# Block-sparse attention and a routed expert layer on one core: where v's neighbour rows come from, and what is loaded ahead of an expert's weights

## The chip, the cores and the metric

The kernel runs on one core of a Trainium2 chip. The metric is device time in microseconds, the median of several executions; lower is better. One execution in each run is recorded by the hardware profiler, and the profile and trace quoted here are of that execution.

A core has TensorE (PE in the profile, its weight loads PEld), VectorE (DVE), ScalarE (ACT), GpSimd (POOL) and SyncE (SP). Transfers run on 16 DMA engines. In this kernel POOL issues every load from HBM that also converts fp32 to bf16, and SP issues the stores of the output.

## The reference

There are 4 batches, 8 heads, 768 positions and a head size of 64. Attention comes first. Each query sees the keys closer than 16 positions, and 24 summary keys, each the maximum over a block of 32 keys, whose value is the mean of the block:

```python
k_sum = k.reshape(B, H, nb, block, D).max(axis=3)
v_sum = v.reshape(B, H, nb, block, D).mean(axis=3)
scores_l = scale * np.matmul(q, k.transpose(0, 1, 3, 2))
mask_l = np.abs(pos[:, None] - pos[None, :]) < window        # window = 16
scores_s = scale * np.einsum('bhsd,bhnd->bhsn', q, k_sum) + np.log(block)
scores_all = np.concatenate([np.where(mask_l, scores_l, -1e9), scores_s], axis=-1)
a = softmax(scores_all)
attn = np.matmul(a, np.concatenate([v, v_sum], axis=2))
```

The heads are joined to x of 768 x 512 for each batch. Then one of 8 experts is chosen per batch, by the mean of x over its positions, and applied:

```python
logits = x.mean(axis=1) @ w_gate
e_idx = np.argmax(logits, axis=1)
h = np.maximum(x[b] @ w1[e], 0.0)          # 512 x 1024
out[b] = gate_w[b] * (h @ w2[e])           # 1024 x 512
```

So the weights of a batch can be fetched only when its attention is done.

## The kernel before

**Layout.** A batch is worked on in 4 pairs of heads, and a pair in 2 halves of 384 positions. The positions of a head lie in 12 blocks of 64. For each block the 64 queries are multiplied with 120 key rows: the block's own 64, 16 neighbours before (`R_PRE`), 16 behind (`R_POST`), and the 24 summaries (`R_SUM`). Bias matmuls with `mbias` and `ends` put a large negative number on what lies outside the window and on the neighbours that a head's first and last block do not have. `kaug` holds the keys in this form, `vblk` the values: rows 0 to 63 the block, 64 to 95 the two strips of neighbours, 96 to 119 the block sums, with extra columns of ones (32 for the sums) that give the denominator. Both exist twice, and batches alternate. `edges(i)` fills the constant parts.

**The steps.** `T_k` and `T_q` transpose a pair's keys and queries on TensorE (L241), and copies put them into `kaug` and `qT`. `K_rest` computes on DVE the block maxima (L271), the neighbour columns and the summary columns. `S_tile` does the biases (L350) and scores (L362), then the exponential on ACT (L372). `V_sum` sums v over blocks with matmuls (L300), `V_copy` spreads the sums over `vblk` on DVE (L315). `O_tile` multiplies weights and values (L386), then divides on DVE (L394, L397). `X_tile` transposes the result into `xT` (L413), and ACT sums its positions while it copies (L414). `gate(b)` computes the logits (L427), the maximum and its index, has POOL read the index, and issues the loads of w1 in four pieces (L453: 128, 128, 256 and 512 of 1024 columns) and w2 in two (L457). `H_chunk` is one 128 x 384 tile of the hidden layer (L492, 16 in a batch); `O_chunk` is half of a 128 x 512 output tile (L515, 12 in a batch), and every second one ends with a scaled copy and a store by SP (L531).

`warm` (L229) issues matmuls on zeros. `first_warm` has nine of 512 columns at the start; in batch 0 each score tile has two of 384 columns ahead of it, each output tile one, each sum two of 128.

**The order.** Nothing is planned by a tool: every engine works through its instructions in the order in which the program emits them. Batch 0 goes pair by pair (`a0`): transposes, sums, scores, outputs. From then on `weave(main, fill)` emits the chunks of one batch's expert layer with the attention steps of the next spread evenly between them: output chunks of batch b-1 with `scores(b + 1)`, hidden chunks of b with `values(b + 1)`, then `gate(b + 1)`. `values` starts with all sums and all four `V_copy`.

**The loads.** POOL's queue is in program order as well. At the start it holds keys, queries and values of batch 0 by pairs, then keys and queries of batch 1. The neighbour rows of batch 0's values are copied inside SBUF by SP, per pair (`halo`, L125 and L129, called from `V_sum`). For the other batches they come from HBM in two loads (`load_halos`, L114 and L118), and `gate` has a slot for them:

```python
nc.gpsimd.dma_start(w1_sb[:, :, fs], w1_src[:, :, fs])   # four pieces of w1
between()              # load_v of the next batch, two loads; load_halos, two
nc.gpsimd.dma_start(w2_sb[:, fs, :], w2_src[:, fs, :])   # two pieces of w2
```

So the order behind gate b is w1 of b, v of b + 1, w2 of b, and then (`load_k`, `load_q`) k and q of b + 2.

## Time and profile before

| | |
|---|---|
| median of 3 runs | 197.66 us (194.01, 206.86, 197.66) |
| the profiled execution, whole | 196.97 us |
| its span, first to last instruction | 194.9 us |
| mean granted TensorE clock | 0.939 |
| read from HBM | 38.00 MB |
| loads by POOL's queue | 19.00 MB as written to SBUF |

The span is what the views of the trace show; 2.07 us lie around it. Times in the views are microseconds from the start of the span. In the lists in order of time, a row has the start, the duration from the first to the last of its instructions, the engine, the line and the operation, the number of instructions, and in brackets the idle time before it and what ended it. A list of waits has for each pair the sum, the number, and the longest. Rows for a load have its size as written and the time from issue to landing.

### The profile page before, as it was taken

What the parts mean: (1) busy time and instruction counts of PE and PEld (TensorE: products, weight loads), DVE (VectorE), ACT (ScalarE), POOL (GpSimd) and SP (SyncE); (2) the same over time, 40 slices, a digit from 0 to 9 for tenths busy, and PEclk for the clock granted to TensorE, in tenths of its full rate; (3) what the DMA queues carried; (4) which work ended last, traced back from release to release, by engine and by line L of the source; (5) the groups of instructions that cost most, each with busy time, mean ns of one, the idle gap of its engine ahead of it and who ended that gap; (6) DMA issues with size and microseconds to landing.
All of it is one profiled execution on the core that took longest, in us unless ns stands there. A gap on an engine that the chain in (4) does not pass through costs nothing.

```text
span 194.9 us, 5234 instructions
## 1 busy us (share of the span) xinstructions
PE 165.7 (85%) x2242; PEld 95.9 (49%) x2257; DVE 92.6 (47%) x249; ACT 91.8 (47%) x187; POOL 47.1 (24%) x65
## 2 busy tenths in 40 slices
PE   7497988859987698989959998799969989979991
PEld 2355556547444365455525565455635644545440
DVE  5625475475036463768214853975257533121211
ACT  2132656748764066265831555466634651436120
POOL 7980000049700000497000000990000008000000
PEclk9998599975699799999996999999999999999999
DMA  4999950019999996399999991799998016999142
GB/s 45 149 172 222 215 93 3 0 20 139 158 101 95 203 207 120 57 151 187 194 123 200 206 175 62 111 157 203 177 157 148 3 55 105 168 274 156 54 161 108
DMA packets 57382, 26.00 MB, mean 133 GB/s; under 512 B 39696, under 2 KB 54288, under 8 KB 57360
## 3 DMA queue, kind: packets, MB, share of 16 engines
q0 software_dynamic: 52992, 19.00, 112.4%
q1 hardware_dynamic: 4368, 6.68, 11.4%
q8 instruction: 17, 0.28, 0.6%
q14 instruction: 5, 0.04, 0.1%
HBM read 38.00 MB, written 6.29 MB: 227 GB/s over the span
## 4 chain that ended last, share of the span: by engine, by line
DMA 36%; PE 35%; POOL 8%; issue 8%; DVE 5%; ACT 4%; POOLq 2%; SPq 0%; DVEq 0%; ACTq 0%
DMA vblk<-in_v_dram 27%; PE hps L492 12%; PE o_ps L515 8%; DMA w_sb<-in_moe_w_dram 6%; PE ops L386 5%; DMA vblk<-vblk 3%; POOL w_sb L453 3%; POOL vblk L104 3%; PE xps L413 2%; ACT xT L414 2%; PE vsps L300 2%; PE sc L229 1%; ACT qT L250 1%; ACT o_sb L530 1%; POOLq L439 1%
## 5 line engine op out<-in xcount | busy, mean ns | idle before, releaser
L492 PE MATMUL hps<-xT,w_sb 128*128 128x384 bf16 x256 | 50.7, 344 | 1.5 <-DMA w_sb<-in_moe_w_dram 1.3
L515 PE MATMUL o_ps<-w_sb,hT 128*128 128x512 bf16 x177 | 43.9, 380 | 1.6 <-issue 1.3
L453 POOL DMA_DIRECT2D w_sb<-in_moe_w_dram x16 | 12.0, 760 | 115.4 <-DVE grec L468 55.3
L503 ACT ACTIVATE hT<-hps 128x384 bf16<-128x384 f32 x48 | 23.4, 493 | 34.4 <-PE hps L492 34.1
L372 ACT ACTIVATE aT<-sc 128x768 bf16<-128x768 f32 x32 | 25.7, 811 | 16.1 <-PE sc L362 16.0
L492 PEld LDWEIGHTS <-w_sb 128*128 128x128 bf16 x256 | 23.6, 101 | 18.0 <-issue 3.1
L515 PEld LDWEIGHTS <-hT 128*128 128x128 bf16 x192 | 16.6, 98 | 17.3
L501 DVE TENSOR_SCALAR hT<-hps 128x384 bf16<-128x384 f32 x16 | 8.9, 558 | 26.6 <-PE hps L492 26.6
L250 ACT COPY qT<-qps 128x768 bf16<-128x768 bf16 x16 | 12.8, 797 | 14.2 <-PE qps L241 14.1
L414 ACT ACTIVATE xT<-xps 128x384 bf16<-128x384 bf16 x32 | 15.6, 489 | 7.1 <-PE xps L413 6.9
L525 DVE TENSOR_SCALAR o_sb<-o_ps,gcol 128x512 f32<-128x512 f32 x12 | 9.0, 751 | 20.5 <-PE o_ps L515 20.5
L397 DVE TENSOR_TENSOR xs<-ops,rv 128x384 bf16<-128x384 f32 x32 | 17.8, 558 | 1.1
L394 DVE RECIPROCAL rv<-ops 128x6 f32<-128x6 f32 x32 | 6.2, 193 | 22.4 <-PE ops L386 22.4
L386 PE MATMUL ops<-vblk,aT 120*64 120x65 bf16 x384 | 11.9, 202 | 5.5 <-DMA vblk<-in_v_dram 4.1
L530 ACT ACTIVATE o_sb<-o_ps,gcol 128x512 f32<-128x512 f32 x12 | 8.3, 688 | 17.2 <-PE o_ps L515 11.3
L362 PE MATMUL sc<-qT,kaug 64*128 64x64 bf16 x384 | 12.4, 204 | 4.2 <-DVE kaug L283 4.2
L271 DVE TENSOR_REDUCE kmx<-kps 128x24 bf16<-128x768 bf16 x16 | 15.1, 945 | 0.1
L386 PEld LDWEIGHTS <-aT 120*64 120x64 bf16 x384 | 8.7, 113 | 12.3 <-issue 8.3
L362 PEld LDWEIGHTS <-kaug 64*128 64x128 bf16 x384 | 9.2, 105 | 6.9 <-DVE kaug L283 5.0
L300 PE MATMUL vsps<-vblk,bind 64*32 64x128 bf16 x192 | 7.7, 231 | 5.7 <-DMA vblk<-in_v_dram 5.7
L413 PE MATMUL xps<-identb,xs 128*128 128x128 bf16 x96 | 10.3, 225 | 2.3 <-ACT qT L250 1.8
L104 POOL DMA_DIRECT2D vblk<-in_v_dram x10 | 12.1, 1228 | 0.0
(74 smaller groups left out, 181.2 us busy)
## 6 DMA issues: line engine op xcount, KB each, us to landing
w_sb<-in_moe_w_dram POOLq DMA_DIRECT2D x12, 512.0 KB, 16.5
out_dram<-o_sb SPq DMA_DIRECT2D x24, 256.0 KB, 5.0
k_nat<-in_k_dram POOLq DMA_DIRECT2D x3, 768.0 KB, 22.7
q_nat<-in_q_dram POOLq DMA_DIRECT2D x3, 768.0 KB, 25.0
vblk<-in_v_dram POOLq DMA_DIRECT2D x6, 384.0 KB, 13.5
vblk<-in_v_dram POOLq DMA_DIRECT2D x6, 190.0 KB, 17.5
w_sb<-in_moe_w_dram POOLq DMA_DIRECT2D x8, 128.0 KB, 4.1
w_sb<-in_moe_w_dram POOLq DMA_DIRECT2D x4, 256.0 KB, 6.2
```

Source lines behind the costliest of these rows:

```text
L104: nc.gpsimd.dma_start(vb[0:QB, h0:h1, :, 0:D].rearrange("p h j d -> p (h j) d"), v[b, h0:h1].rearrange("h (j p) d -> p (h j) d", p=QB),)
L250: nc.scalar.copy(out_, in_)
L271: nc.vector.tensor_reduce(out=kmx, in_=kpss.pop((b, pr)).rearrange("q r (n p) -> q n r p", n=NB), axis=AX.XY, op=ALU.max,)
L362: nc.tensor.matmul(sc[:, hh, w * QB : (w + 1) * QB], lhsT=ka[rs, pr, j, :], rhs=qT[rs, j * QB : (j + 1) * QB], start=False, stop=w == NW - ...
L372: nc.scalar.activation(aT, sc[:, :, 0:HB], ACT.Exp, scale=SCALE)
L386: nc.tensor.matmul(ops[w * QB : (w + 1) * QB, t, hh, :], lhsT=aT[0:NR, hh, c0 : c0 + QB], rhs=vb[0:NR, 2 * pr + hh, u * NW + 2 * t + w, 0 ...
L397: nc.vector.tensor_tensor(out=xs, in0=ops[:, :, :, 0:D], in1=rv.unsqueeze(3).to_broadcast([128, NW // 2, 2, D]), op=ALU.mult,)
L414: nc.scalar.activation(xT[b][:, pr, u * HB : (u + 1) * HB], xps, ACT.Copy, accum_out=red[b][:, pr, u : u + 1],)
L453: nc.gpsimd.dma_start(w1_sb[:, :, fs], w1_src[:, :, fs])
L492: nc.tensor.matmul(hps[:, 0:HB], lhsT=w1_sb[:, dt, ft * 128 : (ft + 1) * 128], rhs=xT[b][:, dt, u * HB : (u + 1) * HB], start=(dt == 0), s ...
L503: nc.scalar.activation(dst, hps[:, 0:HB], ACT.Relu)
L515: nc.tensor.matmul(o_ps, lhsT=hTs[b][:, ft, st * 128 : (st + 1) * 128], rhs=w2_sb[:, ft, :], start=(ft == 0), stop=(ft == NFT - 1),)
```

## The change

- For batch 0, v's neighbour rows come from HBM too. `load_halos` takes a range of heads, and `load_vp` loads v and neighbour rows of one pair: three loads a pair, where there were one load and two copies by SP. The rows of neighbours at a head's ends then hold rows of the next head, which the bias excludes; `clear_ends` zeroes only the first head's first and the last head's last block.
- At the start POOL's queue has k and q of pairs 0 and 1 first, then v of pair 0, then the iotas, and then the rest by pairs.
- k, q, v and neighbour rows of batch 1 are issued ahead of gate 0; those of batch b + 2 right behind the weights of gate b, so ahead of the weights of gate b + 1. `gate` has no slot any more.
- The constant parts of the second `vblk` and `kaug` are filled by POOL, ahead of batch 1's loads, and no longer by DVE.
- Batch 0 is emitted in stages: stage i holds keys, queries and scores of pair i, the output tiles of pair i-1, the transposes of pair i-2 and the sums of pair i. Warm matmuls: two for the first half of each score and output tile pair, none for the second half, none for the sums.
- `values` has each `V_copy` right before its pair's first output tile.
- Two hidden chunks and four output chunks of a batch are emitted behind the next gate; so twelve output chunks, not ten, stand between the last gate and its first hidden chunk.

```diff
+    def load_halos(b, h0=0, h1=H):
...
+        n0, n1 = h0 * NJ, h1 * NJ
+        a, z = max(n0, 1), min(n1, H * NJ - 1)
         nc.gpsimd.dma_start(
+            vb[R_PRE : R_PRE + HALO, a:n1, 0:D],
+            rows[(a - 1) * QB : (n1 - 1) * QB].rearrange("(n p) d -> p n d", p=QB)[
+                QB - HALO : QB
+            ],
+        )
...
-    def halo(b, h0, h1):
-        vb = vblks[b % NV]
-        nc.sync.dma_start(
-            vb[R_PRE : R_PRE + HALO, h0:h1, 1:NJ, :],
-            vb[QB - HALO : QB, h0:h1, 0 : NJ - 1, :],
-        )
...
+    def load_vp(b, pr):
+        load_v(b, 2 * pr, 2 * pr + 2)
+        load_halos(b, 2 * pr, 2 * pr + 2)
+
+    def clear_ends(i, eng):
+
+        eng.memset(vblks[i][QB:R_SUM, 0:1, 0:1, 0:D], 0.0)
+        eng.memset(vblks[i][QB:R_SUM, H - 1 : H, NJ - 1 : NJ, 0:D], 0.0)
...
     load_k(0, 0, 2)
+    clear_ends(0, nc.vector)
...
     load_q(0, 0, 2)
-    load_v(0, 0, 2)
-    load_v(0, 2, 4)
+    load_k(0, 2, 4)
+    load_q(0, 2, 4)
+    load_vp(0, 0)
     it_b = const.tile([QB, NJ, BLK], I32, name="it_b")
...
+    load_vp(0, 1)
+    load_k(0, 4, 6)
+    load_q(0, 4, 6)
+    load_vp(0, 2)
+    load_k(0, 6, 8)
+    load_q(0, 6, 8)
+    load_vp(0, 3)
+
+    def load_vs(b):
+        load_v(b, 0, 4)
+        load_v(b, 4, 8)
+        load_halos(b)
+
+    def load_all(b):
+        load_k(b)
+        load_q(b)
+        load_vs(b)
...
     def V_sum(b, prs):
         def f():
             vb = vblks[b % NV]
-            if b == 0:
-                halo(b, 2 * prs[0], 2 * prs[-1] + 2)
             vs_ps = one_pool.tile([128, 2, D], FP32, name="vsps", tag="one")
-            if b == 0:
-                warm(vs_ps.rearrange("p h c -> p (h c)"), 2, 128)
...
-            if b == 0:
+            if b == 0 and u == 0:
                 warm(sc[:, 0], 2)
...
-            if b == 0:
-                warm(ops.rearrange("p t h c -> p (t h c)"), 1)
+            if b == 0 and u == 0:
+                warm(ops.rearrange("p t h c -> p (t h c)"), 2)
...
-    a0 = [first_warm, T_k(0, 0), *pair_keys(0)]
-    for pr in range(NP):
-        more = pr + 1 < NP
-        a0 += [S_tile(0, pr, 0), S_tile(0, pr, 1)]
-        a0 += [T_k(0, pr + 1)] if more else []
-        a0 += [O_tile(0, pr, 0), O_tile(0, pr, 1)]
-        a0 += pair_keys(pr + 1) if more else []
-        a0 += [X_tile(0, pr, 0), X_tile(0, pr, 1)]
+    a0 = [first_warm]
+    for i in range(NP + 2):
+        if i < NP:
+            a0 += [T_k(0, i), T_q(0, i), K_rest(0, i)]
+        if i >= 2:
+            a0 += [X_tile(0, i - 2, 0), X_tile(0, i - 2, 1)]
+        if i < NP:
+            a0 += [S_tile(0, i, 0), S_tile(0, i, 1)]
+        if 1 <= i <= NP:
+            a0 += [V_copy(0, i - 1), O_tile(0, i - 1, 0), O_tile(0, i - 1, 1)]
+        if i < NP:
+            a0 += [V_sum(0, [i])]
...
     def values(b):
-        st = [V_sum(b, list(range(NP)))] + [V_copy(b, pr) for pr in range(NP)]
+        st = [V_sum(b, list(range(NP)))]
         units = [(pr, u) for pr in range(NP) for u in range(2)]
         for i in range(len(units) + 2):
             if i < len(units):
+                if units[i][1] == 0:
+                    st.append(V_copy(b, units[i][0]))
                 st.append(O_tile(b, *units[i]))
...
-    run(a0[:20])
-    edges(1)
-    run(a0[20:])
-    gate(0, lambda: load_vs(1))
-    load_k(2)
-    load_q(2)
+    clear_ends(1, nc.gpsimd)
+    edges(1, nc.gpsimd)
+    load_all(1)
+    run(a0)
+    gate(0)
+    load_all(2)
     s1 = scores(1)
-    run(s1[:14])
...
-    weave(hs[0][0:6], s1[14:])
-    run(hs[0][6:8])
-    weave(hs[0][8:16] + os_[0][0:2], values(1))
-    gate(1, lambda: load_vs(2))
-    load_k(3)
-    load_q(3)
+    run(s1[:16])
+    weave(hs[0][0:4], s1[16:])
+    weave(hs[0][4:14], values(1))
+    gate(1)
+    load_all(3)
+    run(hs[0][14:16])
+    run(os_[0][0:4])
     for b in range(1, B):
         if b < B - 1:
-            weave(os_[b - 1][2:12], scores(b + 1))
-            run(hs[b][0:5])
-            weave(hs[b][5:16] + os_[b][0:2], values(b + 1))
-            gate(b + 1, (lambda: load_vs(3)) if b == 1 else (lambda: None))
+            weave(os_[b - 1][4:12] + hs[b][0:2], scores(b + 1))
+            run(hs[b][2:4])
+            weave(hs[b][4:16], values(b + 1))
+            gate(b + 1)
+            run(os_[b][0:4])
         else:
-            run(os_[b - 1][2:])
+            run(os_[b - 1][4:])
             run(hs[b])
     run(os_[B - 1])
```

More of the change, by code (lines that the diff above doesn't have):

```diff
@@ L422, with gate @@
     wts = {}
-    def gate(b, between=lambda: None):
+    def gate(b):
         lgps = one_pool.tile([128, 512], FP32, name="lgps", tag="one")
@@ L453, in gate @@
             nc.gpsimd.dma_start(w1_sb[:, :, fs], w1_src[:, :, fs])
-        between()
         for c in range(2):
@@ L537, in moe @@
         ]
-    def pair_keys(pr):
-        return [K_rest(0, pr), V_sum(0, [pr]), V_copy(0, pr), T_q(0, pr)]
     def first_warm():
```

45 lines of the change are left out of this document (12 added, 33 removed).

## The prediction

> **What bounds the kernel now.** I read the page first, then the list of waits of TensorE (PE), then its work in order of time, and last the transfers and the clock in narrow stretches.
>
> ```profile
> span 194.9 us, 5234 instructions
> ...
> PE 165.7 (85%) x2242; PEld 95.9 (49%) x2257; DVE 92.6 (47%) x249; ACT 91.8 (47%) x187; POOL 47.1 (24%) x65
> ```
> ```profile
> PE vsps L300 <- DMA vblk<-in_v_dram: 5.7, 3, 2.4
> PE ops L386 <- DMA vblk<-in_v_dram: 4.1, 2, 3.0
> ```
>
> PE is the only engine near its limit, and it is idle for 29 us. Ten of those are waits for v. The list in order of time tells where (start, duration, and in brackets the idle time just before):
>
> ```profile
> 20.68 0.84 PE L229 MATMUL sc<-zb 128*128 128x384 bf16 x2
> ...
> 28.22 0.49 PE L229 MATMUL sc<-zb 128*128 128x384 bf16 x2
> ...
> 34.21 0.49 PE L229 MATMUL sc<-zb 128*128 128x384 bf16 x2
> ...
> 36.93 0.38 PE L386 MATMUL ops<-vblk,aT 120*64 120x65 bf16 x12
> ...
> 39.21 0.20 PE L427 MATMUL lgps<-wg_sb,red 128*1 128x8 f32 x2 [0.24 <-ACT xT L414]
> ...
> 46.35 0.85 PE L241 MATMUL qps<-identb,q_nat 96*64 96x96 bf16 x16
> ...
> 47.88 0.85 PE L241 MATMUL kps<-identb,k_nat 96*64 96x96 bf16 x16
> 48.67 1.46 PE L492 MATMUL hps<-xT,w_sb 128*128 128x384 bf16 x4
> ...
> 65.19 0.43 PE L386 MATMUL ops<-vblk,aT 120*64 120x65 bf16 x12 [3.03 <-DMA vblk<-in_v_dram]
> ...
> 78.15 0.20 PE L427 MATMUL lgps<-wg_sb,red 128*1 128x8 f32 x2 [0.28 <-ACT xT L414]
> ...
> 102.43 1.06 PE L300 MATMUL vsps<-vblk,bind 64*32 64x128 bf16 x46 [2.40 <-DMA vblk<-in_v_dram]
> 103.43 3.54 PE L492 MATMUL hps<-xT,w_sb 128*128 128x384 bf16 x12
> ...
> 142.60 0.84 PE L300 MATMUL vsps<-vblk,bind 64*32 64x128 bf16 x46 [0.81 <-DMA vblk<-in_v_dram]
> 143.38 2.12 PE L492 MATMUL hps<-xT,w_sb 128*128 128x384 bf16 x12
> ...
> 146.58 0.38 PE L386 MATMUL ops<-vblk,aT 120*64 120x65 bf16 x12 [1.08 <-DMA vblk<-in_v_dram]
> ...
> 159.34 8.81 PE L515 MATMUL o_ps<-w_sb,hT 128*128 128x512 bf16 x39
> ...
> 174.62 5.37 PE L492 MATMUL hps<-xT,w_sb 128*128 128x384 bf16 x32 [1.28 <-DMA w_sb<-in_moe_w_dram]
> ```
>
> Once per batch the value stage stands still, because its v is queued behind the first weights of the batch before. The same twelve matmuls take 3.54 us at 103.43, right after a wait of 2.40 us, and 2.12 us at 143.38, after a shorter one: an idle stretch is paid a second time in clock. The table by stretches says so too (its columns end with the granted clock, the DMA share and GB/s):
>
> ```profile
> 46.00:48.00 2.00, 2.00 (x52) 1.59 (x48) 2.00 (x5) 1.51 (x3) 2.00 (x2) 0.50 1.21 162
> ...
> 66.00:68.00 2.00, 2.00 (x29) 1.02 (x27) 1.36 (x4) 0.00 (x0) 0.00 (x0) 0.50 1.25 207
> ```
>
> At 66, just behind the wait of 3.03 us, the clock is at half too. At 46 it is at half although PE is busy throughout: there PE does transposes and score matmuls only.
>
> **The transfers.** All loads go through POOL's queue. Its issues around gate 0, and with each the time from issue to landing:
>
> ```profile
> 41.55 3.03 POOL L453 DMA_DIRECT2D w_sb<-in_moe_w_dram  x4 [27.87 <-DVE grec L468]
> ...
> 48.17 0.95 POOL L118 DMA_DIRECT2D vblk<-in_v_dram  x1
> 49.07 1.58 POOL L457 DMA_DIRECT2D w_sb<-in_moe_w_dram  x2
> ...
> 52.04 0.78 POOL L91 DMA_DIRECT2D q_nat<-in_q_dram  x1 [0.60 <-DMA w_sb<-in_moe_w_dram]
> ```
> ```profile
> w_sb<-in_moe_w_dram POOLq DMA_DIRECT2D x1, 512.0 KB, 7.9
> vblk<-in_v_dram POOLq DMA_DIRECT2D x1, 190.0 KB, 16.9
> w_sb<-in_moe_w_dram POOLq DMA_DIRECT2D x1, 512.0 KB, 19.7
> q_nat<-in_q_dram POOLq DMA_DIRECT2D x1, 768.0 KB, 25.0
> ```
>
> The last piece of w1 is issued near 43.8 and lands at 51.7; the last halo lands at 48.17 + 16.9 = 65.1, the last of w2 at about 49.8 + 19.7 = 69.5, q at 52.04 + 25.0 = 77.0. They land in the order of issue, so a load costs the queue the difference: v with its halos (1148 KB) 13.4 us, an expert's w2 (1 MB) 4.4 us, k and q 7.5 us. By bytes I split the 13.4 us into 8.9 for v and 4.5 for the halos. The 0.60 us of q are POOL waiting for the fourth piece of w1, eight issues before it: no more than eight loads seem to be under way.
>
> **The change, part by part.** *v ahead of the weights* (batches 1 to 3): 3.03 + 2.40 + 0.81 + 1.08 = 7.32 us of waits go, if v then lands in time; with the two long ones go their clock losses, 3.54 - 2.12 = 1.42 us measured once and charged for both, 2.84 us. Without these idle times no other engine is late next: DVE is busy for 92.6 us in all, ACT for 91.8.
>
> The Trainium skill ("TensorE: Matmul & The Clock Gate", section "Why this matters for your kernels") asks only that PE gaps between bursts of matmuls stay under about 3 us. By that rule the gap of 2.40 us would have cost no clock, and the sum would be 1.42 us later; the trace shows the half clock after it, so here the measurement decides.
>
> *The prologue.* Batch 0's halos no longer pass through SP from SBUF: eight small loads join POOL's queue, and v and halos of batch 1 stand there before gate 0. What carried these loads before ended with q of batch 1:
>
> ```profile
> 12.91 0.78 POOL L91 DMA_DIRECT2D q_nat<-in_q_dram  x1
> ```
> ```profile
> q_nat<-in_q_dram POOLq DMA_DIRECT2D x1, 768.0 KB, 14.5
> ```
>
> That is 27.4. After the change come 4.5 us of batch 0's halos and 13.4 us of batch 1's v and halos: the queue is clear at 45.3, the first 128 KB of w1 (an eighth of 4.4 us) land at 45.9, the last of it at 49.7. The memsets that move from DVE to POOL stand in front of batch 1's loads, where POOL would wait for landings anyway; I charge nothing. Without that cover the eight of them would cost about 8 x 0.23 = 1.8 us, by the one memset of a tile that POOL has now:
>
> ```profile
> masks.py:197 POOL MEMSET identb<- 128x128 bf16 x1 | 0.2, 229 | 0.0
> ```
>
> *PE's start.* The first key work on DVE follows a chain of constants, and these an iota of POOL. Two key and query loads and two halos now stand in front of that iota, in place of one of two v loads:
>
> ```profile
> 3.44 1.93 POOL L104 DMA_DIRECT2D vblk<-in_v_dram  x2
> ...
> 6.91 0.64 POOL L91 DMA_DIRECT2D q_nat<-in_q_dram  x1
> ```
> ```profile
> 8.83 0.94 DVE L271 TENSOR_REDUCE kmx<-kps 128x24 bf16<-128x768 bf16 x1
> ```
>
> Two loads of 0.64 us and two halos (no such small one is in the trace; 0.64 us, the smallest load here, to the 0.95 us of the large halo) less 0.97 us make 1.6 to 2.2 us. I take 1.9, so the reduction moves to 10.7 and the first pair's scores, behind it and three short copies, to about 12.2. From there the new order is denser: pair 0's stage holds no output tile, so pair 1's scores come near 16.5, where they were at 20.68. A pair then took 28.22 - 20.68 = 7.54 us at half clock and 34.21 - 28.22 = 5.99 us at full clock; without the second pair of warm matmuls (0.84 or 0.49 us) that is 6.7 and 5.5. I expect half clock for one more pair, since warm matmuls, scores, outputs and sums of pair 1 follow each other there for nearly 5 us. Then: 16.5 + 6.7 + 5.5, plus 36.93 - 34.21 = 2.7 to the last output tile, 1.5 for the output tiles of the pair before, which now stand in between, and 39.21 - 36.93 = 2.3 to the last gate matmul: gate 0 at 35.2, and at 38 if the clock stays at half.
>
> From that matmul to the first matmul on w1 it was 48.67 - 39.21 = 9.46 us; two steps of scores come ahead of it now, 47.88 - 46.35 = 1.53 us at half clock, so 11.0. The first w1 matmul can start at 35.2 + 11.0 = 46.2, and its weights, in at 45.9, are just not late. It is 48.67 - 46.2 = 2.5 us earlier with 1.5 us more work done: 4.0 us. The bounds are 4.3 (weights the limit) and 1.2 (gate at 38).
>
> *The later queues.* After gate 0 the queue holds w1, w2, k, q, v and halos of batch 2: 4.4 + 4.4 + 7.5 + 13.4 = 29.7 us behind 45.3, so it is clear at 75. Gate 1, at 78.15 before, comes earlier by the 2.5 us of the start, 1.5 of work done ahead, 3.03 + 1.42 of wait and clock, and by two hidden-layer and two output chunks that move behind it (2 x 0.7 and 2 x 0.88 us, below), and later by 1.0 us of the charges below: near 67.5. Its w1 therefore waits for 8 us; but behind gate 1 the two hidden-layer chunks, twelve output chunks (39 matmuls, of ten chunks, take 8.81 us) and the scores of batch 2 come first, well over 12 us. I charge nothing; without that cover it would be 8 us a gate.
>
> *The end.* Twelve output chunks instead of ten stand between gate 3 and its first w1 matmul. Each is 0.88 us, and the two, 1.76, cover the 1.28 us of wait. All other matmuls are the same ones, moved across gates, at no cost.
>
> *Copies of the sums.* They were made ahead of the output tiles and now stand right before each pair's first tile:
>
> ```profile
> L397 DVE TENSOR_TENSOR xs<-ops,rv 128x384 bf16<-128x384 f32 x32 | 17.8, 558 | 1.1
> ...
> L315 DVE COPY vblk<-vs_sb 24x1536 bf16<-24x1536 bf16 x16 | 8.9, 554 | 0.5
> L394 DVE RECIPROCAL rv<-ops 128x6 f32<-128x6 f32 x32 | 6.2, 193 | 22.4 <-PE ops L386 22.4
> ```
>
> Where a copy is queued behind the tile before, the next tile waits for 0.19 + 0.56 + 0.55 = 1.3 us less the chunk of 2.12 / 3 = 0.7 us that stands between: 0.6. By the weave's counts that falls on one pair in four, and I charge 0.5 us for each of three batches, 1.5; the bounds are 0 and 12 x 0.6 = 7.2. Another 0.5 us is for a later return to full clock near 46.
>
> **Sum.** 7.32 + 2.84 + 4.0 + 1.28 - 1.5 - 0.5 = 13.4 us. The profiled execution took 196.97 us, 2.07 more than its span; 194.9 - 13.4 + 2.07 = 183.6. The median of the runs shown, 197.66, is 0.35% above the profiled one: 184.2.
>
> **Rivals.**
>
> *The prologue stays at half clock.* Half of the score stage's warm matmuls and all of the sums' are removed, and the row at 46 shows that a busy PE alone does not bring the clock back. Against it stand the 5 us of untransposed work behind 16.5. Gate 0 at 38 costs 2.8 us: 187.
>
> *DVE takes over as the late one in the value stage.* All twelve pairs wait for their copy: 7.2 instead of 1.5, so 190. For it: DVE works in order. Against: the weave puts most copies a whole chunk ahead.
>
> *Slower: the halos cost by the transfer, not by the byte.* Eight loads of 48 KB enter the prologue's queue. At x us each instead of 4.5 us together, the first w1 comes at 45.9 + 8x - 4.5, and PE waits for it from 46.2. The 13.4 us above, by transfer and not by byte, give 3.35 us for each of its four loads; with x = 3.35 w1 comes at 68.2, and the time is 184.2 + 22.0 = 206. It is slower than before from x = 2.3. Against it: batch 0's v stands in the same queue in four loads, and the queue was clear at 27.4. Into that time go 2 x 7.5 us of k and q with 8.9 us of v by the byte, and not with 4 x 3.35 us.
>
> The skill's page "DMA: Bandwidth & Descriptors" (section "Rules for kernel authors") speaks against this step: small transfers should be joined, and under 64 KB one pays mostly overhead. An estimate from that page's fixed cost of about 2.0 us for each transfer, if transfers followed one another, gives 8 x 2.0 - 4.5 = 11.5 us more in the queue and a time near 195. The trace speaks against it: fourteen loads were in by 27.4, less than 14 x 2.0 us alone, so the fixed parts overlap.
>
> *It does little,* because loads that are early now make weights late at every gate: three times 3 to 4 us given back, 195.
>
> **Chances.** Forecast 0.58 (own range 181.5 to 186.5), half clock 0.17, DVE 0.08, halos by transfer 0.05, little 0.07, still faster than its range 0.05. From 180.5 to 191.5 lie the first three and some of the last. Runs of this kernel differ by some per cent, so 2% is about what can be told from no change: faster (under 193.7) 0.87, within 0.08, slower 0.05.
>
> **What would show it.** Waits of PE on v gone, above all before the sums and the first output tiles of batches 1 to 3; first w1 matmul near 46; last matmuls of gates 0 and 1 near 35 and 67.5; no wait for w1 after gate 3; clock 1.0 in the value stages. I am wrong if PE waits for w_sb by more than 2 us in all, if gate 0 comes after 39, or if waits of PE on DVE's copies exceed 3 us.

## The result, and the profile after

The kernel after takes 183.62 us (median of 4 runs, 181.91 to 184.97), where the kernel before took 196.94 us beside it (194.01 to 206.86). Single executions of either kernel are now and then some per cent longer, so ratios are taken over the executions within 1.5% of a kernel's fastest: the ratio is 0.938, with a 95% interval of 0.919 to 0.957. That is faster, and the median is 0.6 us from the forecast of 184.2. The profiled execution of after took 183.01 us, with a span of 181.4; the span fell by 13.5 us where the sum said 13.4.

The sum's total is right; several of its terms are not, and that their errors cancel is luck. The page of after first, then its list of waits of PE (us in total, times, longest).

```profile
PE 159.2 (88%) x2229; PEld 93.8 (52%) x2241; DVE 90.9 (50%) x241; ACT 91.5 (50%) x187; POOL 53.4 (29%) x81
```
```profile
PE ops L393 <- DVE vblk L322: 4.7, 8, 1.2
PE sc L369 <- DVE kaug L294: 4.3, 4, 1.4
```

PE's idle time fell by 7.0 us (29.2 to 22.2), and its busy time by 6.5 (165.7 to 159.2), about as much again: some warm matmuls are no longer made, and behind the first w1 matmul, where 5.2 of the 6.5 us fall, the same matmuls have a higher clock (the 256 of the hidden layer went from 50.7 to 48.8 us) and a transpose and a score step, 1.53 us at half clock, have moved ahead of it. No wait for v and none for the weights is left. In their place stands, at the head of the list, the wait for DVE's copies of the sums.

The stretches between the last gate matmuls and the first matmul on w1 tell where the time went. First those of before, then those of after; the columns are start and end, length, busy time of PE, its weight loads, DVE, ACT and POOL (instructions in brackets), the granted clock, DMA share and GB/s. The two stages left out run at clock 1.00 in both. The clocks of the two first rows, 0.91 and 0.77, cannot be set against each other; the last section says why.

```profile
0.00:39.41 39.41, 31.67 (x485) 19.35 (x487) 20.60 (x72) 18.13 (x33) 12.36 (x25) 0.91 0.90 111
39.41:48.67 9.26, 7.23 (x176) 5.76 (x177) 6.70 (x20) 6.27 (x10) 7.12 (x8) 0.61 0.72 83
48.67:78.35 29.68, 24.74 (x340) 14.27 (x340) 11.78 (x30) 15.23 (x36) 3.55 (x5) 0.89 2.38 149
78.35:120.06 41.71, 37.01 (x549) 21.12 (x556) 22.64 (x55) 21.21 (x45) 10.62 (x12) 0.96 1.45 153
...
```
```profile
0.00:37.17 37.17, 28.12 (x469) 18.26 (x470) 19.80 (x64) 17.66 (x33) 23.20 (x45) 0.77 1.81 141
37.17:48.07 10.90, 9.49 (x208) 7.40 (x209) 6.86 (x21) 7.94 (x12) 8.08 (x10) 0.56 2.81 132
48.07:69.14 21.07, 17.72 (x291) 10.69 (x290) 10.97 (x28) 12.56 (x32) 2.56 (x3) 0.99 2.46 171
69.14:108.01 38.87, 36.81 (x558) 21.07 (x563) 23.50 (x56) 21.66 (x46) 10.59 (x12) 1.00 2.28 172
...
```

The last gate matmuls of gates 2 and 3 end at 120.06 and 159.41 in before, at 108.01 and 145.27 in after. Set against the prediction's own steps, stage by stage (moved work is in the predicted column: two hidden-layer and two output chunks leave the stretch ahead of gate 1, 3.16 us; two hidden-layer chunks of them, 1.41 us, lengthen the next stretch, since two output chunks of batch 1 leave that one in turn):

| stage | predicted change (us) | measured | what differs |
|---|---|---|---|
| start to first w1 matmul | -2.5 | -0.6 | gate 0 at 37.0, not 35.2 |
| w1 to gate 1 | -8.1 | -8.6 | copies 2.1 worse; clock and small waits better |
| gate 1 to gate 2 | -1.9 | -2.8 | copies 0.4 worse; clock and small waits better |
| gate 2 to gate 3 | -1.4 | -2.1 | copies 0.4 worse; small waits better |
| gate 3 to end | +0.5 | +0.6 | |
| sum | -13.4 | -13.5 | |

### The profile page after: what moved, and what is told of

It is laid out like the page before. It is cut to its first block, busy times and chain, and to the rows that moved or that the text cites. A ratio compares the mean times of both kernels' runs of the same rounds, so it can differ in the third digit from the quotient of the medians.

```text
span 181.4 us, 5192 instructions
## 1 busy us (share of the span) xinstructions
PE 159.2 (88%) x2229; PEld 93.8 (52%) x2241; DVE 90.9 (50%) x241; ACT 91.5 (50%) x187; POOL 53.4 (29%) x81
## 4 chain that ended last, share of the span: by engine, by line
PE 76%; DVE 12%; ACT 4%; POOL 3%; issue 3%; POOLq 0%; DVEq 0%
PE o_ps L521 23%; PE hps L498 22%; PE ops L393 5%; PE sc L369 4%; PE sc L357 4%; PE kps L252 4%; PE qps L252 4%; PE vsps L307 3%; PE xps L420 3%; DVE vblk L322 2%; DVE xs L404 2%; ACT xT L421 2%; DVE kmx L282 2%; PE ops L240 1%; ACT kaug L261 1%
## 5 line engine op out<-in xcount | busy, mean ns | idle before, releaser
L498 PE MATMUL hps<-xT,w_sb 128*128 128x384 bf16 x256 | 48.8, 328 | 0.0
L521 PE MATMUL o_ps<-w_sb,hT 128*128 128x512 bf16 x180 | 42.5, 380 | 1.5 <-issue 1.3
L498 PEld LDWEIGHTS <-w_sb 128*128 128x128 bf16 x256 | 22.4, 98 | 13.1 <-issue 0.2
L521 PEld LDWEIGHTS <-hT 128*128 128x128 bf16 x192 | 17.3, 98 | 19.3
L393 PEld LDWEIGHTS <-aT 120*64 120x64 bf16 x384 | 8.9, 113 | 13.5 <-DVE vblk L322 7.1
L393 PE MATMUL ops<-vblk,aT 120*64 120x65 bf16 x384 | 11.5, 201 | 4.8 <-DVE vblk L322 4.7
L263 DVE COPY kaug<-kps 128x768 bf16<-128x768 bf16 x10 | 9.5, 951 | 6.2 <-PE kps L252 6.2
L252 PE MATMUL qps<-identb,q_nat 96*64 96x96 bf16 x256 | 10.4, 236 | 2.0 <-DMA q_nat<-in_q_dram 2.0
## 6 DMA issues: line engine op xcount, KB each, us to landing
q_nat<-in_q_dram POOLq DMA_DIRECT2D x3, 768.0 KB, 17.6
```

The lines of the kernel that those rows point to most:

```text
L252: nc.tensor.transpose(ps[hh * D : (hh + 1) * D, r, :], src[:, 2 * pr + hh, r * D : (r + 1) * D], identb[0:PR, 0:PR],)
L393: nc.tensor.matmul(ops[w * QB : (w + 1) * QB, t, hh, :], lhsT=aT[0:NR, hh, c0 : c0 + QB], rhs=vb[0:NR, 2 * pr + hh, u * NW + 2 * t + w, 0 ...
L498: nc.tensor.matmul(hps[:, 0:HB], lhsT=w1_sb[:, dt, ft * 128 : (ft + 1) * 128], rhs=xT[b][:, dt, u * HB : (u + 1) * HB], start=(dt == 0), s ...
L521: nc.tensor.matmul(o_ps, lhsT=hTs[b][:, ft, st * 128 : (st + 1) * 128], rhs=w2_sb[:, ft, :], start=(ft == 0), stop=(ft == NFT - 1),)
```

## Experiments

Each kernel differs from the kernel after by the edit shown, unless it is said otherwise. The times of the kernel before in the runs beside them were 198.52 us (194.52 to 202.25) for the first four (one order of v, the old batch 0, two orders of the copies), 195.83 (one run) for the four that were run once (no warm matmuls, both kernels on the halos, ten chunks the first time), and 200.23 (197.21 to 205.06) for the last four. They and the 196.94 us of the result lie up to 4.4 us apart, so a difference of 1 to 2 us between kernels of different groups decides nothing; there I go by the waits in the traces.

### v behind w1 again, all else as after

```diff
-    gate(0)
-    load_all(2)
+    gate(0, lambda: load_vs(1))
+    load_k(2)
+    load_q(2)
```

The function it takes is called between the loads of w1 and w2. Gates 1 and 2 likewise; ahead of batch 0's work only k and q of batch 1 are loaded.

> The changed kernel with one part undone: v and its halos of the next batch are again issued between w1 and w2 of each gate, k and q behind w2; the prologue and the order of all other work stay as changed. Theory (the gain comes from v being there in time): v lands about 20, 24 and 23 us behind gates 0, 1 and 2 and the halos 26, 29 and 26.5 us, as before the change, while the first output tiles now come 18, 26 and 24 us behind these gates; so TensorE waits for v some 8 + 3 + 2.5 us, half clock follows the long wait, and the time is 193 to 198 us. Rival (the gain comes from the denser prologue and the new order on TensorE, and the place of the loads hardly matters): 184 to 187 us.

Measured: 202.79 us (200.65 to 203.57). By the ratio, counted as in the result, that is 4% slower than the kernel before beside it (against two executions of before only), and it is some 19 us slower than after. The waits for v are the first two rows of its list; then its value stages in order of time:

```profile
PE ops L393 <- DMA vblk<-in_v_dram: 6.9, 3, 2.9
PE vsps L307 <- DMA vblk<-in_v_dram: 4.6, 2, 3.2
```
```profile
57.28 1.46 PE L307 MATMUL vsps<-vblk,bind 64*32 64x128 bf16 x46 [3.16 <-DMA vblk<-in_v_dram]
...
105.11 0.54 PE L393 MATMUL ops<-vblk,aT 120*64 120x65 bf16 x12 [2.92 <-DMA vblk<-in_v_dram]
...
148.21 0.54 PE L393 MATMUL ops<-vblk,aT 120*64 120x65 bf16 x12 [1.98 <-DMA vblk<-in_v_dram]
```
```profile
56.00:66.00 10.00, 6.26 (x93) 3.53 (x93) 3.33 (x9) 0.98 (x2) 0.00 (x0) 0.52 2.28 153
```

The waits come to 11.5 us, near the 13.5 expected; the time, expected at 193 to 198 us, does not fit. Of the 17.6 us of span (199.0 less 181.4) 7.1 are PE's idle time, since other waits shrank by 4.4 us, and 10.5 are its busy time, 169.7 against 159.2 us for the same matmuls; 9.8 of these lie behind the first w1 matmul. There the clock is at half for 10.2, 6.8 and 6.8 us around the waits. So these waits for v cost nearly as much again in clock, and after's weave, which comes to the value stage after four hidden-layer chunks of a batch (before: after eight of the first and five of the others), makes the waits longer than they were (7.32 us in before). The new weave is good only with the new loads.

### The loads and the copies' old place alone

Loads, memsets and their order as after; batch 0's order, the warm matmuls, the place of the copies, the weave and the ten chunks at the end as before. Of the main part:

```diff
-    run(s1[:16])
-    weave(hs[0][0:4], s1[16:])
-    weave(hs[0][4:14], values(1))
+    run(s1[:14])
+    weave(hs[0][0:6], s1[14:])
+    run(hs[0][6:8])
+    weave(hs[0][8:16] + os_[0][0:2], values(1))
     gate(1)
     load_all(3)
...
-            weave(hs[b][4:16], values(b + 1))
+            weave(hs[b][5:16] + os_[b][0:2], values(b + 1))
```

> The kernel of before with the loads alone as in the change: batch 0's halos from HBM, the new order of POOL's queue, the memsets on POOL, k, q and v of the next batch ahead of the weights. The order of all other work, the warm matmuls, the copies of the sums ahead of the output tiles and the ten chunks behind the last gate are those of before. Theory (the loads carry the gain, and the new order costs as much as it brings): no wait for v, the wait for w1 behind the last gate stays, and the time is that of the changed kernel or up to 4 us less, since its waits on copies are missing: 180 to 184.5 us. Rival (both parts are needed; the order of before hides less): 187 to 190 us.

Measured: 185.15 us (184.71 to 191.74), 0.938 of the kernel before (0.929 to 0.947), the same ratio as after, and 0.65 us above the range that the theory expected. So the order of the loads is enough for the whole gain. (The memsets on POOL and batch 0's halos from HBM belong to it here; a run below takes the halos out and loses nothing, the memsets were not tried apart.) Its waits show what the other parts then add and take:

```profile
PE vsps L309 <- DMA vblk<-in_v_dram: 5.4, 1, 5.4
...
PE hps L500 <- DMA w_sb<-in_moe_w_dram: 1.4, 1, 1.4
```

The 5.4 us are batch 0's first sums (the old order makes them before any score), the 1.4 us the w1 of the last gate behind ten chunks. After has neither, and pays 4.7 us for its copies instead.

### Batch 0 in its old order

```diff
-            a0 += [T_k(0, i), T_q(0, i), K_rest(0, i)]
...
+    a0 = [first_warm, T_k(0, 0), *pair_keys(0)]
...
```

The rest of the list and the warm matmuls are those of before too.

> The changed kernel with batch 0's steps in the order of before (sums ahead of the query transposes, output tiles of a pair right behind its scores) and with all warm matmuls of before; the loads stay as changed. Theory: the first sums now wait for v, which stands behind two key and query loads and lands near 12.4 us, so gate 0 comes near 42 instead of 37, the first w1 matmul near 53 instead of 48, and the time is 187 to 190 us. Rival (the weights' place in the queue sets the first w1 matmul): at most 1 us more, 183 to 185 us.

Measured: 184.63 us (182.39 to 186.36); span 180.7. The time is the rival's; its reason is not what the trace shows:

```profile
11.35 1.43 PE L309 MATMUL vsps<-vblk,bind 64*32 64x128 bf16 x12 [4.97 <-DVE kaug L291]
...
37.01 0.19 PE L436 MATMUL lgps<-wg_sb,red 128*1 128x8 f32 x2 [0.23 <-ACT xT L423]
```
```profile
16.00:17.00 1.00, 1.00 (x33) 0.85 (x29) 0.00 (x0) 0.47 (x1) 1.00 (x3) 0.88 1.98 148
```

PE stands for 5 us ahead of the first sums, as the theory had it (the trace lays the end of it to DVE's key rows and not to v), and still has gate 0's last matmul at 37.01, as after does (36.97). Nor do the weights set the first w1 matmul: the first piece landed at 44.6, 3 us ahead of it (47.65). But in this trace the clock is full from 16.2 on, in after from 24.7 on. In these 8.5 us after has PE busy for 7.54 us at half clock; if all of that work shortens as the sums do, from 1.46 to 0.84 us, full clock would save some 3 us by this estimate. So what the old order costs may be hidden by the earlier clock. The run above with the old order (loads alone) has its full clock from 16.7, and whether the additional warm matmuls bring that about or chance does was not tried. Shown is only that the new order brings nothing to the gate in this pair of traces.

### No warm matmuls in the stages of batch 0

```diff
-                warm(sc[:, 0], 2)
+                pass
-                warm(ops.rearrange("p t h c -> p (t h c)"), 2)
+                pass
```

> The changed kernel without the warm matmuls inside batch 0's stages (two ahead of each pair's first score tile, two ahead of its first output tile); the nine at the start stay. In the changed kernel the clock returns to full near 24.8 us. Theory: it needs a stretch of 3.4 us in which TensorE does little but matmuls that are not transposes; without the warm ones there is none in batch 0, the clock stays at half until the first w1 matmuls, and gate 0 comes at 38 to 40 instead of 37.0, although 16 matmuls of 0.2 to 0.4 us are gone. Rival (a busy TensorE is enough): the clock returns as before, and gate 0 comes near 35.

Measured: 182.7 us, one run, span 181.0.

```profile
24.00:36.00 12.00, 10.89 (x200) 8.96 (x200) 7.35 (x19) 6.53 (x14) 1.44 (x2) 0.50 2.58 169
```
```profile
38.09 0.20 PE L434 MATMUL lgps<-wg_sb,red 128*1 128x8 f32 x2 [0.24 <-ACT xT L421]
...
48.11 0.82 PE L498 MATMUL hps<-xT,w_sb 128*128 128x384 bf16 x4
```

The clock stays at half through the whole stage, although PE is busy for 10.89 of 12 us. Gate 0 is only 1.1 us later than in after, since at full clock PE waits for DVE and ACT instead (in after it is busy for 7.42 of the 10 us between 26 and 36, at clock 1.00). And the first matmul on w1 comes at 48.11, as in after (48.07). That is luck of the clock: here it came back at 46.1, in after at 48.7, so that the last two rounds of transposes and scores took 2.0 us, where two such rounds take 3.07 us at half clock. In this one run the stage's half clock costs 1.1 us at the gate; that it costs nothing at w1 in general is not shown.

### The iotas ahead of the second key loads

On the copies-first kernel below: the POOL iotas stand right behind the first query load, ahead of pair 1's loads and the first v.

```diff
     load_q(0, 0, 2)
-    load_k(0, 2, 4)
-    load_q(0, 2, 4)
-    load_vp(0, 0)
     it_b = const.tile([QB, NJ, BLK], I32, name="it_b")
...
+    load_k(0, 2, 4)
+    load_q(0, 2, 4)
+    load_vp(0, 0)
```

> The changed kernel with all copies of the sums ahead of the output tiles, and with the iotas ahead of the second pair's key load in POOL's queue. In the changed kernel DVE waits 3.99 us for the iota and the first scores start at 11.56. Theory: the constants are done 3 us earlier, the query copy becomes the limit, and the first scores start near 9.6; gate 0 comes 1 to 2 us earlier; the first w1 matmul is then held by its weights near 45 to 46, so 1 us is gained over the copies alone: 178 to 179.5. Rival (nothing of the prologue reaches the end): 179.5 to 180.5.

Measured: 181.77 us (178.79 to 182.43).

```profile
9.06 0.51 PE L369 MATMUL sc<-qT,kaug 64*128 64x64 bf16 x12 [0.16 <-DVE kaug L294]
...
12.10 1.44 PE L307 MATMUL vsps<-vblk,bind 64*32 64x128 bf16 x12 [1.89 <-DMA vblk<-in_v_dram]
```

The first scores come 2.5 us earlier (9.06, after: 11.56), the sums behind them then wait for v, and gate 0's last matmul is where it was (36.77, after: 36.97). The time lies above both expectations (178 to 179.5 and 179.5 to 180.5). The shift of the iota that the prediction charged on PE's start is real and ends at the next wait.

The same with four warm matmuls of 512 columns between the first key and query transposes:

```diff
+            a0 += [T_k(0, i)] + ([fill_warm] if i == 0 else [])
```

> As the run before, and four warm matmuls of 512 columns between the first key transposes and the first query transposes, where TensorE waits 2.0 us for q. Theory: they cost at most 0.3 us, and the clock returns to full one or two spells of 3.4 us earlier in batch 0 than at 25; at half clock such a spell is worth up to 1.7 us at gate 0, of which the weights of gate 0, in near 45, leave less than 1 us: 177 to 179.5. Rival (the clock does not return earlier): as the run before.

Measured: 181.04 us (179.3 to 181.78), 0.916 of before (0.900 to 0.932). Gate 0 came at 35.24 in its trace, the earliest of all, and the first w1 matmul at 47.55, only 0.5 us ahead of after: the clock fell to half at 33.8, where in after it did at 38.4. No gain over the copies-first kernel (179.77) can be told.

### Twice as many halo loads, and none

The first kernel loads the halos of batch 0 head by head, sixteen loads of 24 KB instead of eight of 48 KB; the second copies them from SBUF on SP's queue, as the kernel before did, so that POOL's queue has none of them (with `halo` and its memsets as they were before).

```diff
     def load_vp(b, pr):
         load_v(b, 2 * pr, 2 * pr + 2)
-        load_halos(b, 2 * pr, 2 * pr + 2)
+        load_halos(b, 2 * pr, 2 * pr + 1)
+        load_halos(b, 2 * pr + 1, 2 * pr + 2)
```

> The changed kernel with each of batch 0's eight halo loads cut into two by heads: sixteen loads of 24 KB for eight of 48 KB, the same rows. If halos cost by the byte, the last halo of batch 1 lands where it did, at 44.4 us, within 1 us, and the first w1 piece at 45.1. If they cost by the transfer, each of the eight more costs what one cost, 4.5 / 8 = 0.6 us by my split or more: 49 us and later, and the first w1 matmul, at 48.1 so far, waits for its weights.

```diff
     def load_vp(b, pr):
         load_v(b, 2 * pr, 2 * pr + 2)
-        load_halos(b, 2 * pr, 2 * pr + 2)
...
     def V_sum(b, prs):
         def f():
             vb = vblks[b % NV]
+            if b == 0:
+                halo(b, 2 * prs[0], 2 * prs[-1] + 2)
```

> The changed kernel with batch 0's halos copied inside SBUF by SyncE again, two copies a pair that are issued when that pair's v has landed. Theory: POOL's queue is shorter by what the eight halo loads cost, so batch 1's last halo lands near 40 instead of 44.4; gate 0 and the first w1 matmul do not move, since TensorE and not the queue sets them: the time is as of the changed kernel within 1 us (183 to 184). Rival (the eight loads slow the prologue): gate 0 earlier by 1 us or more.

Measured: 187.7 us with sixteen, 183.81 with none, one run each. What counts is when the last halo of batch 1, the end of the queue ahead of w1, lands. Of each kernel the row of its issue, from the list in order of time, and the row of the DMA issues with the time to landing: first after, then with sixteen, then with none.

```profile
25.41 0.94 POOL L121 DMA_DIRECT2D vblk<-in_v_dram  x1
```
```profile
vblk<-in_v_dram POOLq DMA_DIRECT2D x1, 190.0 KB, 19.6
```
```profile
29.31 0.91 POOL L121 DMA_DIRECT2D vblk<-in_v_dram  x1
```
```profile
vblk<-in_v_dram POOLq DMA_DIRECT2D x1, 190.0 KB, 18.8
```
```profile
19.47 0.91 POOL L121 DMA_DIRECT2D vblk<-in_v_dram  x1 [0.42 <-DMA k_nat<-in_k_dram]
```
```profile
vblk<-in_v_dram POOLq DMA_DIRECT2D x1, 190.0 KB, 22.5
```

The queue is clear at 45.0, 48.1 and 42.0 us. Eight loads cost 3.0 us, or 0.37 each; as many bytes in twice as many loads cost another 3.1, or 0.39 for each load more. So a small load here costs by the load, not by the byte. (Whether that is POOL's time to issue one, 0.55 to 0.63 us, or the transfer, the runs do not tell; and the copies of the last kernel use the same DMA engines.) That the price is small is the point: the "slower" rival needed 2.3 us a load. Without halos in the queue PE's start is not earlier: first w1 matmul at 48.56 (after: 48.07), as the weights were not what it waited for. With sixteen the span is 4.6 us longer, though PE does not wait for w1 there either. Gate 0 is 1.3 us later, a stretch of 1.5 us without a cause in the trace stands ahead of the first w1 matmul (51.27), and the clock stays at half until 54.6, where after has it full from 48.7. These make most of the 4.6 us; why they come in this one run is open.

### The copies ahead of all output tiles, or one pair ahead

```diff
-        st = [V_sum(b, list(range(NP)))]
+        st = [V_sum(b, list(range(NP)))] + [V_copy(b, pr) for pr in range(NP)]
...
-                if units[i][1] == 0:
-                    st.append(V_copy(b, units[i][0]))
```

> The changed kernel with all four copies of the sums ahead of the output tiles again, as before the change. In the changed kernel TensorE waits 4.5 us in batches 1 to 3 for such a copy. Theory: those waits go but for the first of each batch, three more copies of 0.55 us stand ahead of the first divisions, and 2.5 to 4 us are gained: 179.5 to 181 us. Rival: the waits move to the divisions, for which the transposes and the output buffers then wait: 183 to 184 us.

In the second kernel each pair's copy stands behind the first output tile of the pair before it (pair 0's ahead of its own):

```diff
+                if i == 0:
+                    st.append(V_copy(b, 0))
                 st.append(O_tile(b, *units[i]))
+                if units[i][1] == 0 and units[i][0] + 1 < NP:
+                    st.append(V_copy(b, units[i][0] + 1))
```

> The changed kernel with each copy of the sums one output tile earlier: that of pair n+1 between the two tiles of pair n. Theory: a copy is then queued ahead of one division less and has one more chunk of TensorE in front of its tile, so of the 4.5 us of waits on copies at most 1 us is left: 180 to 181 us. Rival as for the copies first: 183 to 184 us.

Measured: 179.77 us (179.16 to 180.5) and 179.77 (178.29 to 181.75), both ahead of after, in separate runs. By the ratio they take 0.922 and 0.918 of before (against two executions of it). The waits for copies in the first (span 177.5), then in the second:

```profile
PE ops L393 <- DVE vblk L322: 0.2, 1, 0.2
```
```profile
PE ops L393 <- DVE vblk L322: 1.3, 5, 0.4
```

Of the 4.7 us in after, 4.5 are gone with the first, and its span is 3.9 shorter. Behind the first w1 matmul, where the edit acts, it is 3.3 us shorter, since 1.3 us of waits for the divided tiles have come in; the rest comes ahead of it, where the clock came back at 46.0 and not at 48.7. So the place of the copies costs somewhat less than the list of waits says. Rid of it, the new weave and order may be worth some 2%: the two kernels with the iotas ahead, which have the copies first, took 181.77 and 181.04 us beside 185.15 for the loads alone. That is about as little as these runs can tell. The copies-first kernel is the best of this study together with its neighbour, and beats both kernels of this case, against after by executions that do not overlap (up to 181.75, from 181.91).

### Ten output chunks again between gate 3 and its w1

```diff
-            weave(hs[b][4:16], values(b + 1))
+            early = 2 if b == 2 else 0
+            weave(hs[b][4:16] + os_[b][0:early], values(b + 1))
             gate(b + 1)
-            run(os_[b][0:4])
+            run(os_[b][early:4])
```

> The changed kernel with two output chunks of batch 2 ahead of the last gate again, so that ten and not twelve stand between it and its first hidden chunk. Theory: the last piece of w1 lands 15.1 us behind the last gate's last matmul; the fifth hidden row would need it 14.2 us behind it, so TensorE waits about 0.9 us there and the time grows by as much. Rival: no wait, since the weights land earlier with nothing else in the queue.

Measured: 190.18 us (one run), span 188.5.

```profile
165.39 8.23 PE L498 MATMUL hps<-xT,w_sb 128*128 128x384 bf16 x32 [3.12 <-DMA w_sb<-in_moe_w_dram]
```

The wait for the last w1 is back, and the 32 matmuls behind it take 8.23 us where a full clock gives 5.37: 3.12 + 2.86 = 6.0 us. Expected were 0.9 us, so the same kernel ran again, timed against before.

> The kernel with ten and not twelve output chunks behind the last gate, timed. The single look gave a wait for w1 of 3.1 us, not 0.9, then half clock, and 190.2 us. If the wait with its clock loss is the kernel's, the time is 187 to 191 us; if the look was an unlucky one, 184 to 185.5 us, the wait being about 1 us.

Measured: 188.63 us (186.27 to 190.2), 0.948 of before (0.931 to 0.965).

```profile
167.50 5.37 PE L498 MATMUL hps<-xT,w_sb 128*128 128x384 bf16 x32 [2.00 <-DMA w_sb<-in_moe_w_dram]
```

This time 2.00 us of wait and no loss of clock; the time is in the range that was set for a wait that belongs to the kernel. The wait is shown, its price isn't: by the ratios it is 1% slower than after, and the intervals overlap. The weave also changed (fourteen chunks beside the values of batch 3, and 5.3 us of waits for copies), and gate 0, which the edit does not touch, came at 39.80 in this trace. What the two chunks alone are worth stays open between the wait of 2 to 3 us and twice that.

## Why the prediction was right

**Waits for v: right.** They are gone, as the list of waits shows, and putting v behind w1 again brings 11.5 us of them back. Nothing else was late in their place at the sums. The old order with the new loads gives the same ratio as the whole change (0.938), and the new order with v behind w1 is slower than before (1.04): so the loads, and among them the place of v, are the cause of the gain, and not the order of the other work.

**The clock behind the waits: right in kind, too small.** 2.84 us were charged, less 0.5 for a later return near 46. In the stretches, before lost 0.11 of 29.68 us and 0.04 of 41.71 us to half clock, about 3.3 and 1.7 us (one less the clock, times the length); after loses 0.2 and 0. That is 4.7 us instead of 2.34. What I missed is the half clock that lasted until 51.7 in before, 3 us into the first w1 matmuls; in after it ended at 48.7 instead of coming later.

**Start of PE: the wrong step.** Gate 0 was put at 35.2 and came at 36.97. The rows of after, in order of time:

```profile
11.56 0.50 PE L369 MATMUL sc<-qT,kaug 64*128 64x64 bf16 x12 [1.41 <-DVE kaug L294]
...
15.45 0.82 PE L240 MATMUL sc<-zb 128*128 128x384 bf16 x2
...
17.66 0.50 PE L369 MATMUL sc<-qT,kaug 64*128 64x64 bf16 x12 [0.96 <-DVE kaug L294]
...
23.72 0.85 PE L240 MATMUL sc<-zb 128*128 128x384 bf16 x2
...
28.38 0.49 PE L240 MATMUL sc<-zb 128*128 128x384 bf16 x2
...
30.08 0.35 PE L369 MATMUL sc<-qT,kaug 64*128 64x64 bf16 x12 [0.94 <-DVE kaug L294]
...
34.01 0.57 PE L393 MATMUL ops<-vblk,aT 120*64 120x65 bf16 x24 [0.25 <-DVE vblk L322]
...
36.97 0.20 PE L434 MATMUL lgps<-wg_sb,red 128*1 128x8 f32 x2 [0.24 <-ACT xT L421]
48.07 1.08 PE L498 MATMUL hps<-xT,w_sb 128*128 128x384 bf16 x4
```

The prediction counted a pair from its first warm matmul (line L240 here). The first pair's scores were early (11.56, predicted 12.2), and so was pair 1 (15.45, predicted 16.5). Then pair 1 took 8.27 us, predicted 6.7, and the next 4.66, predicted 5.5; from there to the row of the last output tiles it was 5.63, predicted 4.2, and from these to the gate 2.96, predicted 2.3. Two things failed. The pair of 7.54 us in before, taken as one at half clock, was at half only until 24.4, for 3.7 us of it; a whole pair at half clock is longer. And PE waited for DVE's key rows (0.96 and 0.94 us), which was in no term, and longer for the divided tiles ahead of the gate than in before (1.4 us in all, 0.55 there). The clock came back at 24.7, as "one more pair" had it. From gate 0 to the w1 matmul it was 11.10 us, predicted 11.0, and there two errors cancel: PE waited 0.99 us for the key rows and not 2.03 as in before, but the clock fell to half at 38.4 and not at 41.5. So this term gave 0.6 + 1.5 = 2.1 us instead of 4.0, inside the bounds of 1.2 and 4.3. Which of the weights or the gate is the limit was a near thing in the prediction (45.9 against 46.2); it is the gate, by 3 us: the first piece of w1 landed at 45.1.

```profile
39.33 3.03 POOL L460 DMA_DIRECT2D w_sb<-in_moe_w_dram  x4 [12.97 <-DVE kaug L263]
```
```profile
w_sb<-in_moe_w_dram POOLq DMA_DIRECT2D x1, 128.0 KB, 5.8
```

**The queue: right as a sum, wrong as a price.** Clear at 45.3 by the prediction, 45.0 measured. The halos of batch 0 were 4.5 us "by the byte" in it; they cost 3.0, and by the load. Without them the queue was clear at 42.0, where the prediction's sum without them is 40.8, so that the total fits is luck. The Trainium skill ("DMA: Bandwidth & Descriptors", section "Rules for kernel authors") has transfers under 64 KB as mostly overhead. That agrees, since halving the loads' size doubled their cost (3.0 and 6.1 us), but 0.37 us a load is far from the 2.0 us that the prediction tried, by an estimate from that page's fixed cost.

**Copies of the sums: the mis-sized term.** Predicted 1.5 us (bounds 0 and 7.2), measured 4.5 in the three batches and 4.7 with batch 0. The prediction called itself wrong if these waits exceeded 3 us; in this term it was. DVE's rows of after, and what PE waits for:

```profile
56.52 0.56 DVE L404 TENSOR_TENSOR xs<-ops,rv 128x384 bf16<-128x384 f32 x1
57.09 0.55 DVE L322 COPY vblk<-vs_sb 24x1536 bf16<-24x1536 bf16 x1
...
63.39 0.56 DVE L507 TENSOR_SCALAR hT<-hps 128x384 bf16<-128x384 f32 x1
63.96 0.56 DVE L322 COPY vblk<-vs_sb 24x1536 bf16<-24x1536 bf16 x1
```
```profile
64.57 0.38 PE L393 MATMUL ops<-vblk,aT 120*64 120x65 bf16 x12 [1.22 <-DVE vblk L322]
```

The wait was seen, its size not: the prediction had a copy queued behind the tile before it on DVE, 0.6 us on one pair in four. In batch 1 the second pair's copy (57.09) stands behind the divisions of both tiles of the first pair, and the fourth pair's (63.96) behind a division and a hidden-layer chunk that DVE takes off PSUM; PE waits 1.20 and 1.22 us for them, and 0.23 on a third pair. Batch 1's weave has ten chunks, not twelve, so that fewer of them lie between a copy and its tile. In batches 2 and 3 it is 0.2 us on one pair and 0.7 on another, 0.9 in each batch.

**What made up for it.** Copies 3.0 us worse and start 1.9 worse; clock 2.4 better. The other 2.6 are mostly small waits that were not charged. So errors of about 5 us each way cancel, and the forecast is nearer than its working deserves. In before PE waited for DVE's key rows by 1.0, 0.5 and 0.7 us in the three stages behind w1; in after all 4.3 us of them lie ahead of the first w1 matmul, so what is gained here is much of what the start lost. No run tried this by itself.

**End: right.** +0.6 measured from gate 3, +0.5 predicted, and no wait for w1. The runs with ten chunks show the wait that twelve avoid, at 1.4 to 3.1 us.

**Rivals.** Half clock is a rival that does come about in the run without stage warms. Gate 0 was then at 38, as the rival had it, but after, at full clock, was at 37.0 and not at 35.2: the difference is 1.1 us, not 2.8, since at full clock PE waits for DVE. DVE as the late engine came true in part, 4.7 us of its 7.2. Halos by the load: right kind, a ninth of the price. Late weights at every gate: no wait for w1 is left in after.

## What to carry to other kernels

Load ahead what the next stage needs first, and put the weights behind it if other work covers them: here the order of one queue was the whole gain. Price a wait for its idle time and then ask for the clock behind it: here the waits of 2.4 us and more all had half clock beside them, and of those from 1.4 to 2.0 us some had it and some had not. Price a step by whether another engine's wait takes the time back before the next fixed point. After such a change look again for who is late: here a 0.56 us copy, placed right before its reader, cost 4.5 us of waits, more than the start of the kernel had won.

## What was not expected of the hardware

The granted clock changes on a grid. The trace of before, in narrow stretches:

```profile
65.40:65.60 0.20, 0.20 (x12) 0.14 (x5) 0.00 (x0) 0.00 (x0) 0.00 (x0) 0.50 1.32 220
...
68.80:69.00 0.20, 0.20 (x4) 0.13 (x3) 0.20 (x1) 0.00 (x0) 0.00 (x0) 1.00 1.16 195
```

Down at 65.4 (the slice ahead has 0.93), when PE is already back at work behind its wait of 3.03 us, and up at 68.8 (the slice ahead has 0.53), 3.4 us later. The other changes of before, near 17.6, 24.4, 41.5 and 51.7, lie multiples of 3.4 us from these. The Trainium skill ("TensorE: Matmul & The Clock Gate", section "Part 1: The HAM clock gate") has a free-running window of 3413 ns, and this agrees. Its safe gap of about 3 us ("Why this matters for your kernels") does not: with v behind w1 the clock fell to half at 104.1, within a wait of 2.92 us, and at 145.1, behind a wait of 1.44 us and ahead of the one of 1.98. The other way round, the waits for w1 of 2.00 us in the second run with ten chunks and of 1.45 us in the run with the loads alone cost no clock. So the length of a wait alone does not decide it in these traces.

The clock column is not complete at the start of a trace. In before it says 1.00 until 17.6, and yet:

```profile
9.04 1.44 PE L300 MATMUL vsps<-vblk,bind 64*32 64x128 bf16 x12 [2.45 <-DMA vblk<-in_v_dram]
```

The same sums take 0.84 us at 25.86, at full clock, and 1.46 in after at 12.63, where the column has 0.50. So before ran at half there too, and the mean clocks of the two kernels, 0.939 and 0.925, say little; the lengths of equal matmuls do.

What brings the clock back isn't settled. The run without stage warms, with no matmul on w1 before 48.11:

```profile
25.60:29.00 3.40, 3.40 (x60) 3.02 (x57) 1.74 (x6) 1.29 (x3) 0.00 (x0) 0.50 1.25 208
...
45.00:46.00 1.00, 1.00 (x32) 0.90 (x26) 1.00 (x2) 0.56 (x1) 1.00 (x2) 0.50 1.35 122
46.00:46.50 0.50, 0.50 (x14) 0.27 (x9) 0.50 (x2) 0.48 (x2) 0.50 (x2) 0.93 1.09 135
```

From 25.6 PE is busy for 3.4 us without a break, and the clock stays at half behind it too; from 41.8 it does transposes and scores without a break, and has the full clock at 46. In before and after the same work left the clock at half until the first w1 matmuls were under way. Over the fourteen traces of this case the clock came back ahead of the first w1 matmul in seven and behind it in seven. So the prediction's reading of its row at 46, that this work does not bring the clock back, holds in half of them.
